# An operand sum of a Strassen-like product moved from VectorE to two DMA transfers

## The chip, the cores and the metric

The kernel runs on one core of one Trainium2 chip. The metric is the device time of one execution in microseconds. The engines are PE (matmul, with PEld for its weight loads), DVE (VectorE), ACT (ScalarE), POOL (GpSimd) and SP (SyncE, which here only issues transfers).

## The reference

An input `x` of 8 batches, 3008 rows and 256 columns goes through the real part of a two-dimensional Fourier transform and then through an MLP-Mixer layer. The last step, the channel mixing, is where the change lies.

```python
def _attn_ref(x):
    X = np.fft.fft(x, axis=1)
    X = np.fft.fft(X, axis=2)
    return X.real.astype(np.float32)

def _moe_ref(x, w_tok1, w_tok2, w_ch1, w_ch2):      # d_tok 256, d_ch 1536
    xt = x.transpose(0, 2, 1)
    h = np.maximum(xt @ w_tok1, 0.0) @ w_tok2
    u = x + h.transpose(0, 2, 1)
    h2 = np.maximum(u @ w_ch1, 0.0) @ w_ch2
    return (u + h2).astype(np.float32)
```

## The kernel before, in words

**Stages of a batch.** `fold` adds and subtracts mirrored rows and columns of `x` (tiles `xp` and `xm`) into `eo`. `front` turns `eo` into `ut`, the mixed tokens `u`, by small matmuls (`pz`, `pw`, `pt`, `py`, `pu`) with evictions on ACT and DVE. Then each batch has 6 chunks `c` of 512 tokens (448 in the last chunk of odd batches, 384 in that of even ones). For every chunk, `mm1` multiplies `ut` by w_ch1 in 12 steps `ct`, each of two 512-column matmuls into a PSUM tile `pc`, and ACT (in some chunks DVE too) evicts `pc` with a ReLU into `c1`. `pc` rotates through three banks.

**The second product.** `c1` times w_ch2 is done one chunk later. In most chunks (`seven(b, c)` true, 41 of 48) it is done by a scheme of seven block products in place of eight. `c1` is seen as four quarters (`quads`: a11, a12, a21, a22), split by channel half and by alternate blocks of 128 tokens. Four operand sums of 128x1536 elements, `s1` to `s4`, are formed on DVE by `sums`, and sums of the weight quarters (`b22`, `t1w` to `t4w`) were formed once on POOL by `weight_sums`. `mm2_seven` issues the products; each is 12 matmuls of 128 columns. Product 2 uses s2 and t2w, product 3 s1 and t1w, product 4 s3 and t3w, product 6 s4 and b22. DVE combines the results with `uT` (a DMA transpose of `ut`, three buffers) into `osb` (two buffers), and SP stores `osb`. The chunks for which `seven` is false are done by `mm2` with plain 256-column matmuls.

**Order of the work.** The schedule is written out by hand; nothing is reordered by a planner. The main loop runs over batches `b`, chunks `c` and steps `ct`; a slot is 12c + ct. In each slot it issues the `mm1` step of this chunk, and, by the tables below, the products and sums of the chunk before (`prev`):

```python
sum_at = {0: 1, 1: 2, 3: 4, 4: 3}
places = {0: 0, 1: -1, 2: 1, 5: 2, 6: 3, 8: 4, 10: 5, 11: 6}
```

Keys are `ct`. So the sum s3 is made at ct 4 and product 4 that uses it comes at ct 8. Between these, `take(nxt, 1)` spreads the 46 steps of the next batch's `front` over the batch. Each engine works through its own instructions in this order[...].

**POOL's fold.** From batch 2 on, `fold(b + 2)` runs on POOL in 26 pieces, 5 or 6 per chunk, all issued at ct 5. Ahead of them, a one-element copy into `hold` reads a sum, so that POOL begins when DVE has made it. When the last piece has been issued, `load_x` issues the loads of the batch after: two direct transfers into `xp` and two gathers into `xm`, all on POOL's queue. Batch 0 is set up differently: its fold and that of batch 1 are on DVE, and `weight_sums` is issued on POOL at slot 1, when w_ch2 (`wc2`) has been loaded.

Tiles of one `tag` with `bufs=1` share one place in SBUF; a new tile of the tag waits until the last reader of the old one is done. s1 to s4 have a tag each.

Of the kernel before, what the change touches and what calls it, by code (L numbers as in the profile page):

```python
# [36 lines left out]
def kernel(  # L37
# [51 lines left out]
    def tt(out_, a, b, op, eng=V):  # L89
        eng.tensor_tensor(out=out_, in0=a, in1=b, op=op)  # L90
# [4 lines left out]
    def act(out_, in_, scale=1.0, func=AFT.Copy, bias=None):  # L95
        kw = {} if bias is None else {"bias": bias}
        nc.scalar.activation(out=out_, in_=in_, func=func, scale=scale, **kw)  # L97
# [547 lines left out]
    def weight_sums():  # L645
        G.tensor_copy(out=wc2[:, :, D:D + 1], in_=wc2[:, :, P:P + 1])
        lo, hi = wc2[:, 0:NH], wc2[:, NH:NCT]
        b12 = lo[:, :, D:P:-1]
        G.tensor_copy(out=b22[:], in_=hi[:, :, D:P:-1])
        tt(t1w[:], b12, lo[:, :, 0:P], AT.subtract, G)  # L650
        tt(t2w[:], b22[:], t1w[:], AT.subtract, G)
        tt(t3w[:], b22[:], b12, AT.subtract, G)
        tt(t4w[:], hi[:, :, 0:P], t2w[:], AT.subtract, G)

    def mm1(b, c, c1, ct, on_v, cts=None):
        ut = state[b]["ut"]
        n = min(CW, S - CW * c)
        cts = cts or (ct,)
        pcs = [ps_out("pc", k % 5) if b + c == 0 and k % 5 < 2 else ps_mm("pc") for k in cts]
        for h in range(2):  # L660
            for pc, ct in zip(pcs, cts):
                nc.tensor.matmul(pc[:, 0:n], lhsT=wc1[:, h, ct * P:(ct + 1) * P],  # L662
                                 rhs=ut[:, c, h, 0:n], start=(h == 0), stop=(h == 1))
        for pc, ct in zip(pcs, cts):
            if ct not in on_v:
                act(c1[:, ct, 0:n], pc[:, 0:n], func=AFT.Relu)
            else:
                ts(c1[:, ct, 0:n], pc[:, 0:n], 0.0, AT.max)

    tail1 = const.tile([P, NCT, 64], FP16, tag="tail1")  # L670

# [21 lines left out]
    def quads(c1):  # L693
# [3 lines left out]
    def sums(c1, box, k):  # L697
        a11, a12, a21, a22 = quads(c1)
        box[k] = work.tile([P, NH, 2, P], FP16, tag=f"s{k}", name=f"s{k}", bufs=1)
        if k == 1:  # L700
            tt(box[1][:], a21, a22, AT.add)
        elif k == 2:
            tt(box[2][:], box[1][:], a11, AT.subtract)
        elif k == 3:
            tt(box[3][:], a11, a21, AT.subtract)
        else:
            tt(box[4][:], a12, box[2][:], AT.subtract)

    def product(dst, left, right, first):
        for a in range(2):  # L710
# [5 lines left out]
    def halves(ps):  # L716
        return ps[:, 0:2 * P].rearrange("p (a r q) -> p a r q", a=2, q=2)

    def mm2_seven(b, c, c1, uT, k, box):
        a11, a12, a21, a22 = quads(c1)  # L720
# [12 lines left out]
        def hi(i):  # L733
            return osb[:, i, :, P + 1:D + 1].rearrange("p a (r q) -> p a r q", q=2)[
                :, :, ::-1, ::-1]

        if k < 0:
            tt(q[:, 0], pa, u[:, 0], AT.add)
        elif k == 1:
            pb = ps_out("pb", 1)  # L740
            product(pb, a12, wc2[:, NH:NCT, 0:P], True)
            tt(lo(0), halves(pb), q[:, 0], AT.add)
        elif k == 2:
            product(box["a"], box[2], t2w, False)
            tt(q[:, 1], pa, u[:, 1], AT.add)
        elif k == 3:
            box["b"] = ps_out("pb", 1)
            product(box["b"], box[1], t1w, True)
        elif k == 4:
            product(box["a"], box[3], t3w, False)  # L750
            tt(q[:, 2], pa, u[:, 3], AT.add)
            tt(hi(1), halves(box["b"]), q[:, 2], AT.add)
        elif k == 5:
            product(box["a"], a22, t4w, False)
            tt(lo(1), pa, u[:, 2], AT.add)
# [49 lines left out]
    def take(g, n):  # L805
        for _ in range(n):
            next(g, None)
# [48 lines left out]
              36: 1, 39: 1}  # L856
    prev = uT = uT_next = None
    folding = left = 0
    for b in range(BB):
        nxt = front(b + 1) if b + 1 < BB else iter(())  # L860
        fold1 = fold(1, V) if b == 0 and BB > 1 else iter(())
        first, done = (24 if b == 0 else 5 + 12 * ((left + 5) // 6 - 1) if left else 0), 0
        for c in range(NCH):
            c1 = work.tile([P, NCT, CW], FP16, tag="c1", name="c1", bufs=2)
            if c == 5 and b % 2:
                G.tensor_copy(out=c1[:, :, 448:512], in_=tail1[:])
            box = {}
            joins = prev is not None and seven(*prev[0:2])
            on_v = ((1, 5, 8), ())[c] if b == 0 and c < 2 else () if joins else (0, 3, 6, 9)
            for ct in range(NCT):  # L870
                slot = NCT * c + ct
# [77 lines left out]
```

## Time and profile before

| | before |
|---|---|
| median of 3 runs | 601.85 us (601.52 to 602.42) |
| the profiled execution's own time | 601.77 us |
| its span | 599.8 us |
| PE, DVE, ACT, POOL busy | 582.5, 449.5, 390.2, 255.1 us |
| matmuls | 6273 |
| mean granted PE clock | 0.999 |
| moved by DMA | 55.69 MB |

A profile shows one execution. A row of it names the line, the engine, the operation and the tiles, with the time of each instruction, and in the columns after it the idle time of the engine just before and what ended it. Most VectorE and GpSimd additions carry the line of a helper (L90), and most ACT operations that of another (L97), so that tiles tell them apart.

### The profile page before, as it was taken

What the parts mean: (1) busy time and instruction counts of PE and PEld (TensorE: products, weight loads), DVE (VectorE), ACT (ScalarE), POOL (GpSimd) and SP (SyncE); (2) the same over time, 40 slices, a digit from 0 to 9 for tenths busy, and PEclk for the clock granted to TensorE, in tenths of its full rate; (3) what the DMA queues carried; (4) which work ended last, traced back from release to release, by engine and by line L of the source; (5) the groups of instructions that cost most, each with busy time, mean ns of one, the idle gap of its engine ahead of it and who ended that gap; (6) DMA issues with size and microseconds to landing.
All of it is one profiled execution on the core that took longest, in us unless ns stands there. A gap on an engine that the chain in (4) does not pass through costs nothing.

```text
span 599.8 us, 15331 instructions
## 1 busy us (share of the span) xinstructions
PE 582.5 (97%) x6273; PEld 417.8 (70%) x6273; DVE 449.5 (75%) x924; ACT 390.2 (65%) x753; POOL 255.1 (43%) x396
## 2 busy tenths in 40 slices
PE   3899999999999999999999999999999999999997
PEld 3756676677767776667767777677766777666776
DVE  8769879685898668766898668856688757966663
ACT  8764665478647865477656867568665786556662
POOL 8550545937555554626348444565555000000000
PEclk9999999999999999999999999999999999999999
DMA  8992822277138913394335753376133422323533
GB/s 158 207 192 61 170 50 53 61 149 119 37 71 121 149 37 68 78 181 54 68 84 91 135 89 55 67 147 113 37 60 80 93 55 55 77 61 77 93 72 88
DMA packets 83414, 55.69 MB, mean 93 GB/s; under 512 B 53778, under 2 KB 80082, under 8 KB 82578
## 3 DMA queue, kind: packets, MB, share of 16 engines
q1 hardware_dynamic: 76816, 36.82, 31.9%
q0 software_dynamic: 6208, 17.63, 16.2%
q8 instruction: 49, 0.80, 0.6%
q10 hardware_dynamic: 320, 0.26, 0.2%
q14 instruction: 21, 0.17, 0.1%
HBM read 35.26 MB, written 24.64 MB: 100 GB/s over the span
## 4 chain that ended last, share of the span: by engine, by line
PE 82%; DVE 1%; issue 0%; DVEq 0%
PE pc L662 36%; PE pa L712 17%; PE pb L712 13%; PE pu L566 6%; PE po L775 4%; PE pt L595 3%; PE pz L471 1%; PE py L538 1%; PE pw L512 1%; PE pw L508 1%; DVE s L90 1%; DVE osb L90 0%; DVE ut L90 0%; PE pz L496 0%; DVE q L90 0%
## 5 line engine op out<-in xcount | busy, mean ns | idle before, releaser
L97 ACT ACTIVATE c<-pc 128x512 f16<-128x512 f32 (+1 forms) x553 | 314.4, 591 | 156.2 <-PE pc L662 138.7
L662 PE MATMUL pc<-ut,wc 128*128 128x512 f16 (+1 forms) x1152 | 316.5, 374 | 1.2 <-DVE ut L90 1.2
L712 PEld LDWEIGHTS <-s 128*128 128x128 f16 x1968 | 123.5, 98 | 37.5 <-DVE s L90 0.6
L662 PEld LDWEIGHTS <-wc 128*128 128x128 f16 x1152 | 97.0, 98 | 50.7 <-issue 3.0
L712 PEld LDWEIGHTS <-c 128*128 128x128 f16 x1476 | 93.0, 97 | 27.8
L90 DVE TENSOR_TENSOR q<-pa,uT 128x256 f32<-128x256 f32 x123 | 52.5, 427 | 47.6 <-PE pa L712 47.5
L90 DVE TENSOR_TENSOR s<-c 128x1536 f16<-128x1536 f16 x82 | 80.7, 984 | 4.7 <-ACT c L97 4.7
L908 POOL COPY hold<-s 128x1 f16<-128x1 f16 x29 | 5.4, 187 | 173.5 <-DVE s L90 173.5
L90 DVE TENSOR_TENSOR osb<-pb,q 128x256 f32<-128x256 f32 x123 | 52.0, 422 | 23.8 <-PE pb L712 20.3
L90 DVE TENSOR_TENSOR ut<-pu,yt 128x512 f16<-128x512 f32 (+1 forms) x96 | 63.3, 672 | 0.8 <-PE pu L566 0.4
L90 POOL TENSOR_TENSOR eo<-sab 96x512 f16<-96x512 f16 x48 | 52.7, 1114 | 1.6
L566 PE MATMUL pu<-w2r,uu 128*128 128x512 f16 (+1 forms) x168 | 50.0, 379 | 0.3 <-DVE ut L90 0.3
L90 POOL TENSOR_TENSOR sab<-fa,fb 96x256 f16<-96x256 f16 (+1 forms) x72 | 46.7, 673 | 0.0
L90 DVE TENSOR_TENSOR s<-s,c 128x1536 f16<-128x1536 f16 x41 | 40.4, 986 | 0.0
L97 ACT ACTIVATE w<-pw 128x257 f16<-128x257 f32 x90 | 34.8, 387 | 8.4 <-PE pw L512 5.5
L90 DVE TENSOR_TENSOR s<-c,s 128x1536 f16<-128x1536 f16 x41 | 39.0, 952 | 0.0
L775 PE MATMUL po<-wc,c 128*128 128x256 f16 x288 | 35.4, 273 | 0.0
L712 PE MATMUL pb<-wc,c 128*128 128x128 f16 x492 | 34.4, 219 | 0.0
L712 PE MATMUL pa<-wc,c 128*128 128x128 f16 x492 | 34.4, 219 | 0.0
L712 PE MATMUL pa<-t2w,s 128*128 128x128 f16 x492 | 34.2, 219 | 0.1
L712 PE MATMUL pb<-t1w,s 128*128 128x128 f16 x492 | 34.2, 219 | 0.0
L712 PE MATMUL pa<-t4w,c 128*128 128x128 f16 x492 | 34.2, 219 | 0.0
(187 smaller groups left out, 728.0 us busy)
## 6 DMA issues: line engine op xcount, KB each, us to landing
out_dram<-osb SPq DMA_DIRECT2D x83, 256.0 KB
xp<-in_x_dram POOLq DMA_DIRECT2D x14, 408.0 KB, 6.4
out_dram<-osb SPq DMA_DIRECT2D x11, 192.0 KB
uT<-ut SPq DMA_TRANSPOSE x96
w2n<-in_moe_w_tok_dram POOLq DMA_DIRECT2D x2, 752.0 KB, 9.8
w1p<-in_moe_w_tok_dram POOLq DMA_DIRECT2D x2, 384.0 KB, 8.2
wc<-in_moe_w_ch_dram POOLq DMA_DIRECT2D x1, 768.0 KB, 15.3
xp<-in_x_dram POOLq DMA_DIRECT2D x2, 272.0 KB, 5.7
```

Of the source, the lines that this page charges most:

```text
L90: eng.tensor_tensor(out=out_, in0=a, in1=b, op=op)
L97: nc.scalar.activation(out=out_, in_=in_, func=func, scale=scale, **kw)
L471: nc.tensor.matmul(out_, lhsT=rows[:, half * P:half * P + P], rhs=tab, start=True, stop=True)
L508: nc.tensor.matmul(pw[:, 0:256].rearrange("p (h d) -> p h d", h=2)[:, :, 0:65], lhsT=zg[:, 0, g], rhs=td[:, 0:130].rearrange("p (h d) -> p ...
L512: nc.tensor.matmul(pw[:, 64:322].rearrange("p (h d) -> p h d", h=2)[:, :, 0:64], lhsT=zg[:, 1, g], rhs=td[:, 130:258].rearrange("p (h d) - ...
L538: nc.tensor.matmul(py[:, P * k:P * k + P], lhsT=w[:, 4 * c + k, o:o + P], rhs=tab[:, 4 * c + k, :], start=True, stop=True)
L566: nc.tensor.matmul(pu[:, 0:64 * nk], lhsT=uu[:, th, h, :], rhs=w2[:, th, :, 8 * c:8 * c + nk], start=(th == 0), stop=(th == 1))
L595: nc.tensor.matmul(pt[:, o:o + n], lhsT=hw[:, g, c], rhs=w[:, g, w0:w0 + n], start=(g == 0), stop=(g == NG - 1))
L662: nc.tensor.matmul(pc[:, 0:n], lhsT=wc1[:, h, ct * P:(ct + 1) * P], rhs=ut[:, c, h, 0:n], start=(h == 0), stop=(h == 1))
L712: nc.tensor.matmul(dst[:, P * a:P * a + P], lhsT=left[:, k, a, :], rhs=right[:, k, :], start=(first and k + a == 0), stop=(k == NH - 1), s ...
L775: nc.tensor.matmul(po[:, o:o + D], lhsT=c1[:, ct, ks * P:ks * P + P], rhs=wc2[:, ct, 0:D], start=(ct == 0), stop=(ct == NCT - 1))
L908: G.tensor_copy(out=hold[:], in_=pbox[3][:, 0, 0, 0:1])
```

## The change

It has five parts.

1. **The third sum by transfers.** For chunks with c below 5 in batches 1 to 7 (`by_dma`, 35 chunks), s3 is no longer made by DVE. `sum_start` issues on SP, at ct 7 of the chunk's own turn, a copy of a11 into s3; `sum_end` issues on POOL, at ct 9, a transfer that adds a21 into it. The sum is then used, as before, at ct 8 of the next chunk's turn. For the other six chunks of the scheme s3 stays on DVE.
2. **Signs.** [...]s2, s3 and s4 become sums where they were differences. The weight sums and the results change sign with them. `t2w` is now minus `t4w`'s first form: `weight_rest`, at slot 10 of batch 0, makes it by an ACT copy with scale -1, and then POOL subtracts a quarter of w_ch2 from `t4w`.
3. **Layout.** For chunks with c below 5 that use the scheme, `c1` is written so that each quarter is one contiguous run of 1536 elements in a partition (`blocked`). Evictions write, and products and sums read, through that view.
4. **Places.** s3 of the next chunk is now filled while s1 to s3 of the chunk before are in use. The three tags rotate (`homes`): the new s3 takes the place of the old s1, which product 3 reads last, at ct 6.
5. **POOL's order.** The fold's pieces of a chunk are halved: one half at ct 5, the other at ct 9, behind `sum_end`. `load_x` comes behind that second half. In the chunk after a load (`late_x`), from batch 2 on, 4 pieces are taken in place of 5; the last piece of the fold then falls in chunk 0 of the next batch. `hold` reads s4 in place of s3.

```diff
 def weight_sums():
-        tt(t1w[:], b12, lo[:, :, 0:P], AT.subtract, G)
-        tt(t2w[:], b22[:], t1w[:], AT.subtract, G)
+        tt(t1w[:], lo[:, :, 0:P], b12, AT.subtract, G)
         tt(t3w[:], b22[:], b12, AT.subtract, G)
-        tt(t4w[:], hi[:, :, 0:P], t2w[:], AT.subtract, G)
+        tt(t4w[:], lo[:, :, 0:P], t3w[:], AT.add, G)
+
+    def weight_rest():
+        act(t2w[:], t4w[:], scale=-1.0)
+        tt(t4w[:], t4w[:], wc2[:, NH:NCT, 0:P], AT.subtract, G)
...
+            if seven(b, c) and c < NCH - 1:
+                dst = blocked(c1)[:, :, ct].rearrange("p i a t -> p a i t")
+                src = pc[:].rearrange("p (a i t) -> p a i t", a=2, i=2)
...
+    homes = [1, 2, 3]
+
+    def new_sum(box, k):
+        t = homes[k - 1] if k < 4 else 4
+        box[k] = work.tile([P, NH, 2, P], FP16, tag=f"s{t}", name=f"s{k}", bufs=1)
...
         elif k == 3:
-            tt(box[3][:], a11, a21, AT.subtract)
+            tt(box[3][:], a11, a21, AT.add)
...
+    def sum_start(c, c1, box):
+        homes.append(homes.pop(0))
+        new_sum(box, 3)
+        nc.sync.dma_start(out=box[3][:], in_=quads(c, c1)[0])
+
+    def by_dma(b, c):
+        return c < NCH - 1 and b > 0
+
+    def sum_end(c, c1, box):
+        G.dma_start(out=box[3][:], in_=quads(c, c1)[2], accum_op=AT.add)
...
-                    if ct in sum_at:
-                        sums(prev[2], pbox, sum_at[ct])
+                    k = sum_at.get(ct, 3)
+                    if ct in sum_at and (k != 3 or not by_dma(*prev[0:2])):
+                        sums(*prev[1:3], pbox, k)
...
+                if by_dma(b, c):
+                    if ct == 7:
+                        sum_start(c, c1, box)
+                    if ct == 9:
+                        sum_end(c, c1, box)
                 if slot == 1 and b == 0:
                     weight_sums()
+                if slot == 10 and b == 0:
+                    weight_rest()
...
                         if joins:
-                            G.tensor_copy(out=hold[:], in_=pbox[3][:, 0, 0, 0:1])
-                        n = min(left, 6 if c == 5 or b < 2 else 5)
-                        take(fold2, n)
+                            G.tensor_copy(out=hold[:], in_=pbox[4][:, 0, 0, 0:1])
+                        n = min(left, 6 if c == 5 or b < 2 else 4 if late_x else 5)
+                        take(fold2, n - n // 2)
                         left -= n
-                        if left == 0 and folding + 1 < BB:
-                            load_x(folding + 1)
+                        late_x = False
+                if ct == 9 and n:
+                    take(fold2, n // 2)
+                    n = 0
+                    if left == 0 and folding + 1 < BB:
+                        load_x(folding + 1)
+                        late_x = True
```

More of the change, by code (lines that the diff above doesn't have):

```diff
@@ L664, in mm1 @@
         for pc, ct in zip(pcs, cts):
+            if seven(b, c) and c < NCH - 1:
+                dst = blocked(c1)[:, :, ct].rearrange("p i a t -> p a i t")
+                src = pc[:].rearrange("p (a i t) -> p a i t", a=2, i=2)
+            else:
+                dst, src = c1[:, ct, 0:n], pc[:, 0:n]
             if ct not in on_v:
-                act(c1[:, ct, 0:n], pc[:, 0:n], func=AFT.Relu)
+                act(dst, src, func=AFT.Relu)
             else:
-                ts(c1[:, ct, 0:n], pc[:, 0:n], 0.0, AT.max)
+                ts(dst, src, 0.0, AT.max)
     tail1 = const.tile([P, NCT, 64], FP16, tag="tail1")
@@ L691, in store, with blocked, quads, sums @@
                 in_=osb[64:128, 3, 0:D])
-    def quads(c1):
+    def blocked(c1):
+        return c1[:].rearrange("p c n -> p (c n)").rearrange(
+            "p (i c a t) -> p i c a t", i=2, c=NCT, a=2)
+    def quads(c, c1):
+        if c < NCH - 1:
+            v = blocked(c1)
+            return v[:, 0, 0:NH], v[:, 0, NH:NCT], v[:, 1, 0:NH], v[:, 1, NH:NCT]
         v = c1[:].rearrange("p c (a i t) -> p c a i t", a=2, i=2)
         return (v[:, 0:NH, :, 0], v[:, NH:NCT, :, 0], v[:, 0:NH, :, 1], v[:, NH:NCT, :, 1])
-    def sums(c1, box, k):
-        a11, a12, a21, a22 = quads(c1)
-        box[k] = work.tile([P, NH, 2, P], FP16, tag=f"s{k}", name=f"s{k}", bufs=1)
+    homes = [1, 2, 3]
+    def new_sum(box, k):
+        t = homes[k - 1] if k < 4 else 4
+        box[k] = work.tile([P, NH, 2, P], FP16, tag=f"s{t}", name=f"s{k}", bufs=1)
+    def sums(c, c1, box, k):
+        a11, a12, a21, a22 = quads(c, c1)
+        new_sum(box, k)
         if k == 1:
@@ L702, in sums @@
         elif k == 2:
-            tt(box[2][:], box[1][:], a11, AT.subtract)
+            tt(box[2][:], box[1][:], a11, AT.add)
         elif k == 3:
-            tt(box[3][:], a11, a21, AT.subtract)
+            tt(box[3][:], a11, a21, AT.add)
         else:
-            tt(box[4][:], a12, box[2][:], AT.subtract)
+            tt(box[4][:], a12, box[2][:], AT.add)
+    def sum_start(c, c1, box):
[6 more added lines that the diff above has]
+        G.dma_start(out=box[3][:], in_=quads(c, c1)[2], accum_op=AT.add)
     def product(dst, left, right, first):
@@ L719, in mm2_seven @@
     def mm2_seven(b, c, c1, uT, k, box):
-        a11, a12, a21, a22 = quads(c1)
+        a11, a12, a21, a22 = quads(c, c1)
         u = uT[:].rearrange("p (a i) h (q r) -> p (i h) a r q", a=2, q=2)
@@ L750, in mm2_seven @@
             product(box["a"], box[3], t3w, False)
-            tt(q[:, 2], pa, u[:, 3], AT.add)
-            tt(hi(1), halves(box["b"]), q[:, 2], AT.add)
+            tt(q[:, 2], u[:, 3], pa, AT.subtract)
+            tt(hi(1), q[:, 2], halves(box["b"]), AT.subtract)
         elif k == 5:
             product(box["a"], a22, t4w, False)
-            tt(lo(1), pa, u[:, 2], AT.add)
+            tt(lo(1), u[:, 2], pa, AT.subtract)
         elif k == 6:
@@ L858 @@
     folding = left = 0
+    n, late_x = 0, False
     for b in range(BB):
```

## The prediction

> **What bounds the kernel now.** I read the page's first part, then who waits for PE, then busy time in windows, and last the timelines of two places that the change touches.
>
> The page's busy times (share of the span, instructions) come first; under them, from the page's chain, the shares by engine:
>
> ```profile
> PE 582.5 (97%) x6273; PEld 417.8 (70%) x6273; DVE 449.5 (75%) x924; ACT 390.2 (65%) x753; POOL 255.1 (43%) x396
> ...
> PE 82%; DVE 1%; issue 0%; DVEq 0%
> ```
>
> The waits of PE alone (total us, times, longest):
>
> ```profile
> PE filler L399 <- DVE ident L84: 8.1, 1, 8.1
> PE pc L662 <- DVE ut L90: 1.2, 2, 0.9
> ```
>
> Two windows of 100 us (busy us of PE, PEld, DVE, ACT, POOL; clock; DMA share; GB/s):
>
> ```profile
> 0.00:100.00 100.00, 87.03 (x853) 60.67 (x854) 83.19 (x225) 66.12 (x131) 53.19 (x82) 1.00 0.71 131
> ...
> 200.00:300.00 100.00, 100.00 (x1122) 73.17 (x1120) 73.28 (x142) 67.87 (x134) 50.03 (x78) 1.00 0.49 84
> ```
>
> PE is the bound, and from 100 us on it is busy without a gap. A busy PE is not proof of pace, so I compared starts: back-to-back matmuls start 0.216 us apart for 512 columns and 0.056 us for 128. Beyond that pace PE loses some 3 us in all after 100 us. No edit removes a matmul, so 3 us is the most that any relief of another engine can give there. What can move the time much is a new wait of PE.
>
> **What the Trainium skill says.**
> - "DMA: Bandwidth & Descriptors", section "SWDGE vs HWDGE vs iDMA": accumulating is only possible on a transfer issued by GpSimd. That is why POOL must issue the second transfer, in order with its fold. No accumulating transfer is in this trace.
> - The same page, "Anatomy of one DMA — SWDGE (gpsimd) path": about 2.0 us plus bytes over 436 GB/s, 2.9 us for the 393 KB here (128 partitions of 3,072 bytes). The trace disagrees: 408 KB of xp take a median 6.4 us to land. The trace decides.
> - "Collectives: The Full Stack", "The bandwidth ceiling: the fold count and why AG ≠ RS ≠ AR": an add inside a transfer needs two source reads, so it moves at about half the rate of a copy. Not shown here; it sets my upper bound.
> - "SBUF — State Buffer", "Who interferes with whom": a VectorE instruction with two SBUF inputs and a GpSimd one that reads SBUF exclude each other. The trace agrees: an operand sum takes 0.95 us alone and up to 1.49 us beside GpSimd's `pad` operations.
>
> **Part 1: weights (once).** One of POOL's subtractions becomes an ACTIVATE of `t2w` from `t4w`, at slot 10 of batch 0. ACT is in order: the evictions of slots 11 and later stand behind it, and PE has three banks for `pc`. POOL's timeline of before, then ACT's:
>
> ```profile
> 36.83 0.23 POOL L646 COPY wc<-wc 128x12 f16<-128x12 f16 x1 [5.92 <-DMA wc<-in_moe_w_ch_dram]
> 37.13 0.82 POOL L649 COPY b<-wc 128x768 f16<-128x768 f16 x1
> 37.92 1.50 POOL L90 TENSOR_TENSOR t1w<-wc 128x768 f16<-128x768 f16 x1
> 39.50 1.64 POOL L90 TENSOR_TENSOR t2w<-b,t1w 128x768 f16<-128x768 f16 x1
> 41.10 1.51 POOL L90 TENSOR_TENSOR t3w<-b,wc 128x768 f16<-128x768 f16 x1
> ```
>
> ```profile
> 39.19 3.05 ACT L97 ACTIVATE c<-pc 128x512 f16<-128x512 f32 x6 [0.21 <-PE pc L662]
> ```
>
> POOL starts only when w_ch2 lands, at 36.83 us. Afterwards it runs b22, t1w, then t3w (39.50 to 41.0) and the first form of t4w (41.1 to 42.8, at the 1.72 us of today's t4w). ACT has evicted slot 10 at 40.3 and waits until 42.8. The copy itself takes 0.83 us (ACT's 768-element rows from SBUF are 832 and 934 ns): 43.7. Slot 11's eviction, begun at 40.16 today, ends at 44.3 (0.60 us each). PE's matmul for slot 14 needs that bank; it starts at 40.94 today, so PE is **3.4 us** late.
>
> Not all of it stays. DVE is behind PE here, because it folds batch 1 in the same stretch:
>
> ```profile
> 44.22 1.50 PE L775 MATMUL po<-wc,c 128*128 128x256 f16 x12
> ```
>
> ```profile
> 46.63 0.74 DVE L90 TENSOR_TENSOR osb<-po,uT 128x256 f32<-128x256 f32 x2
> ```
>
> The first DVE instruction that needs delayed PE work, `osb` at 46.63, has its input at 45.7. So 0.9 us is absorbed and DVE is 2.5 us late. From there DVE runs without a gap to the `ut` that PE waits for before chunk 2 (the 1.2 us above), with over 1 us of room at each later input. Everything behind follows: **+2.5 us**, bounds 0 (below nothing is excluded: nothing is removed from PE or ACT here) and 3.4. POOL's last subtraction, after the copy, hides behind some 16 us of free POOL time.
>
> **Part 2: the sum that DVE loses.** 35 chunks (c below 5, batches 1 to 7) lose one `s<-c` each: 35 x 0.95 = 33 us of DVE. It is off the path: PE waited for a sum 0.6 us in the whole run. Gain 0 to 1 us; I take 0. The blocked layout of c1, the swapped signs and the added access dimensions keep the element counts: evictions stay at 0.60 us, sums at 0.95. If they did slow, ACT at 65% and DVE at 75% cover them, so 0; a tenth more on each eviction would still leave ACT below PE's time.
>
> **Part 3: the transfers.** Each of those chunks issues, one chunk ahead, a copy on SP (slot 7) and an accumulating transfer on POOL (slot 9). The copy waits for ACT's first six evictions and for the t1w product that last reads the tile it reuses. Behind it on SP stand the uT transposes and the stores, which have most of a chunk to spare (uT is used a chunk and a half later, osb has two tiles). The accumulating transfer waits for the copy's landing; behind it on POOL stand the second half of the fold and the loads of x. The budget is tightest in batch 7, whose chunks are 9.9 us long:
>
> ```profile
> 556.51 0.83 PE L712 MATMUL pb<-t1w,s 128*128 128x128 f16 x12
> ...
> 567.93 0.83 PE L712 MATMUL pa<-t3w,s 128*128 128x128 f16 x12
> ```
>
> The copy can go at 557.3. SP's stores of 256 KB land a median 3.4 us after their issue by the completion records, so I put the copy's landing at 560.8. The t3w product needs the sum at 567.8: the accumulating transfer has **7.0 us**. By the same count the other chunks leave 8.1 us (c=1), 8.3 (c=0), 9.2 (c=3) and 10.7 or more (c=2, 4). Its time is unknown: from below 3.4 us, as a copy; from above 10 us, xp's 6.4 with a second read of some 2 us and a store in the way. I take 6, so nothing is late and the cost is 0.
>
> Moved with it: x is loaded behind the transfer (its 4 issues on POOL, two of 0.54 and two of 0.95 us). In batches 2 to 5 the load falls in c=0 near 10 us, the first gather lands some 8 us later, and the fold of c=1 waits for it; with two fold pieces (2.5 us) ahead, that chunk's accumulating transfer goes 0 to 3 us later than the copy allows. Against 8.1 us of room: 0 to 1 us, four times; I take 0.7 in all. Fold pieces that now run past the chunk's end can meet DVE's first sum (up to 0.5 us each, the 1.49 above); DVE gained 0.95 us per chunk and the t2w product leaves the sums 0.4 to 3 us, so 0.
>
> **Sum.** The profiled execution took 601.77 us (span 599.8, 2.0 around it), 0.08 below the median of the runs. 601.77 + 2.5 + 0 + 0.7 = **605.0 us**.
>
> **Rivals.**
> 1. The accumulating transfer is late in every short chunk. For it: two reads, and stores and transposes share its engines (DMA share 0.34 to 0.5). Against: xp lands in 6.4 us beside other loads. At 9 us batch 7 is short by 2 us per chunk (half of that on average, since a stall lengthens the next budget: 5 us), c=0 and c=1 by 0.8 (about 6 us): 615. At 10 us, 628.
> 2. Not slower: the t2w wait costs nothing. Place: slot 14 of batch 0. It decides once POOL's t4w is ready about 2.6 us sooner, so that PE's delay falls under the 0.9 us that DVE's lag takes up; an earlier landing of w_ch2 than 36.8 us would do that. Price 2.5 us back: 602.5 or, with the loads harmless, 601.8. Against: nothing ahead of that landing is changed.
> 3. DVE's relief shows: PE loses its small waits after 100 us, up to 3 us, and part 1 is absorbed too: about 600. Against: those waits are mostly not for DVE.
>
> **Numbers.** Forecast 0.64, rivals 0.23, 0.10 and 0.03. About 0.2% (1.2 us) is what a measurement of this kernel tells from no change. Slower by more: 0.64 + 0.23 = 0.87; within: 0.10; faster: 0.03. The range, 602.6 to 616, takes in part 1 from 0.9 us up and the accumulating transfer up to 9 us; it leaves out rival 3, most of rival 2 and the upper half of rival 1.
>
> **What would show it.** Right: ACT shows a wait of some 2.5 us for POOL's t4w ahead of `t2w`, PE a hole near 41 us, DVE about 33 us less busy with 35 fewer sums, and no wait of PE (or its weight load) for a DMA into `s`. Wrong: PE waits for `s<-c` transfers in batch 7 or in c=1 (rival 1), or no hole near 41 us (rival 2).

## The result and the profile after

The changed kernel takes **623.12 us** (median of 4 runs, 622.5 to 625.33) against 601.8 us: a ratio of **1.0353** with a 95% interval of 1.0324 to 1.0383. It is slower, as forecast, but by 21 us and not by 3, and the time lies above the range. The profiled execution is the longest of the four, 625.33 us.

The lines of the profile after that answer to those of before. First the page's busy times (share of the span, instructions), then PE's waits (total us, times, longest), then the two windows of 100 us in the same columns as before:

```profile
PE 589.7 (95%) x6273; PEld 419.8 (67%) x6273; DVE 433.4 (69%) x889; ACT 389.0 (62%) x754; POOL 305.0 (49%) x433
```

```profile
PE pa L747 <- DMA s<-c: 9.2, 4, 3.0
PE filler L399 <- DVE ident L84: 8.8, 1, 8.8
PE pa L747 <- DVE s L90: 6.1, 8, 3.0
```

```profile
0.00:100.00 100.00, 86.80 (x850) 60.06 (x851) 83.31 (x225) 66.46 (x131) 54.77 (x82) 1.00 0.69 129
200.00:300.00 100.00, 93.66 (x1005) 67.44 (x1003) 61.85 (x119) 60.91 (x122) 57.05 (x78) 0.97 0.69 145
```

The first 100 us are as before. Behind them PE, which had no gap, waits for the DMA-made sum four times and for DVE's sums eight times, and the clock falls below 1.00. The moved data rose from 55.69 to 83.23 MB. DVE has its 35 sums less and is not awaited less for it.

The length of each chunk, from its first `mm1` matmul to that of the next, says where the loss sits. Against `e17_pairs_late` below, which has the same code but no pair of transfers before batch 6 and makes `t2w` at slot 22, chunk c = 2 of batches 2 to 5 is longer by 4.8, 4.6, 2.2 and 6.3 us (17.8 us together), chunks c = 4 and 5 of these batches by 4.0, batch 1 by 1.1. Batches 6 and 7, whose pairs both kernels have, are not longer; against `e5_rest_later`, which has no pair at all, they are longer by 0.3 us together. Batch 0 isn't longer either, and is within 0.1 us of that of the kernel before.

One of the four chunks, instruction by instruction. POOL's timeline of batch 2 (start, duration, in brackets the idle time before and what ended it), then SP's, then PE's:

```profile
190.79 0.88 POOL L742 DMA_DIRECT2D s<-c  x1 [2.68 <-PE pc L665]
...
192.41 1.33 POOL L106 DMA_DIRECT2D xp<-in_x_dram  x2
194.04 0.97 POOL L109 DMA_INDIRECT xm<-in_x_dram,ix  x1 [0.30 <-issue]
195.32 1.19 POOL L109 DMA_INDIRECT xm<-in_x_dram,ix  x1 [0.30 <-issue]
...
203.39 1.14 POOL L90 TENSOR_TENSOR fa<-xp,xm 96x508 f16<-96x508 f16 x1 [5.59 <-DMA xm<-in_x_dram,ix]
204.50 1.92 POOL L90 TENSOR_TENSOR fb<-xm,xp 96x508 f16<-96x508 f16 x1
206.38 0.95 POOL L90 TENSOR_TENSOR sab<-xp,xm 96x8 f16<-96x8 f16 x1
208.05 0.99 POOL L742 DMA_DIRECT2D s<-c  x1 [0.72 <-PE pc L665]
```

```profile
193.11 1.31 SPq L692 DMA_DIRECT2D out_dram<-osb  x2
194.46 0.61 SPq L697 DMA_DIRECT2D out_dram<-osb  x1
198.80 0.52 SPq L736 DMA_DIRECT2D s<-c  x1
199.37 6.18 SPq L685 DMA_TRANSPOSE uT<-ut  x2
```

```profile
209.50 1.02 PE L665 MATMUL pc<-ut,wc 128*128 128x512 f16 x4
213.48 1.23 PE L747 MATMUL pa<-t3w,s 128*128 128x128 f16 x12 [2.96 <-DMA s<-c]
214.50 0.32 PE L508 MATMUL pw<-td,z 128*128 128x130 f16 x1
```

The completion records of the trace give the landings. Chunk c = 0's accumulating transfer is in place at 194.80. The two loads into `xp` and the two gathers into `xm` (1.6 MB) follow it and land from 198.59 to 205.49. The copy of c = 1 leaves at 198.80, in the midst of them, and lands at **207.46**, after 8.65 us. So the accumulating transfer leaves at 208.05 and lands at 213.43. PE stood before the product that needs the sum from 210.5 on. POOL itself was free at 207.3, so the fold is not what held it: the wait that the row puts down to `pc` ended with the landing of the copy, 0.6 us earlier.

Over all 35 pairs the copy takes a median of 2.83 us and the accumulating transfer 4.47 us; the copies of c = 1 in batches 2 to 5, beside a load, take 7.8 to 9.6 us. In batch 7, whose chunks are the shortest, every sum lands 2.2 to 3.8 us before its product.

The stall is only part of the price. Two windows (busy times as above, clock, DMA share, GB/s), one with the stall and one behind it (a share above 1 comes of counting a packet's whole time where it starts):

```profile
205.90:213.00 7.10, 4.62 (x49) 2.94 (x45) 2.89 (x4) 4.99 (x11) 6.38 (x10) 1.00 1.16 224
213.30:219.00 5.70, 5.52 (x49) 4.08 (x50) 1.38 (x4) 2.46 (x6) 5.32 (x8) 0.70 0.66 99
```

After the stall PE's clock is 0.70 in the mean: matmuls of 128 columns start 0.107 us apart for 3.4 us, in place of 0.056. The stalls of 3.0 to 3.1 us (three of them; counted between the starts of the matmuls on both sides, less their pace, which gives 0.1 to 0.2 us more than the waits in the rows) are each followed by such a stretch, which costs some 1.7 us more; those of 2.1 and 1.6 us are not. The Trainium skill's "TensorE: Matmul & The Clock Gate", section "Part 1: The HAM clock gate", says that the clock halves after an idle window of about 3.4 us; here less was enough. In every profile of this case the recorded clock changes only at points that lie whole multiples of 3.41 us apart, and what tells the cases apart is how much of one such stretch PE stands idle: over all kernels of this document, a stretch of which stalls (those above 0.5 us counted) took 0.64 or more was always followed by the half clock, and one with less than 0.60 never. So a stall of 2.13 us inside one stretch halved the clock (`e7_load_ahead`), and one of 3.08 us across two did not (`e1_five`). The 17.8 us are 13.0 us of waiting and, as the remainder, 4.8 us of slower clock.

### The profile page after: what moved, and what is told of

It is laid out like the page before. It is cut to its first block, busy times and chain, and to the rows that moved or that the text cites. A ratio compares the mean times of both kernels' runs of the same rounds, so it can differ in the third digit from the quotient of the medians.

```text
span 623.6 us, 15583 instructions
## 1 busy us (share of the span) xinstructions
PE 589.7 (95%) x6273; PEld 419.8 (67%) x6273; DVE 433.4 (69%) x889; ACT 389.0 (62%) x754; POOL 305.0 (49%) x433
## 2 busy tenths in 40 slices
DMA packets 93496, 83.23 MB, mean 133 GB/s; under 512 B 54898, under 2 KB 81202, under 8 KB 92658
## 5 line engine op out<-in xcount | busy, mean ns | idle before, releaser
L747 PEld LDWEIGHTS <-s 128*128 128x128 f16 x1968 | 124.3, 99 | 56.4 <-DMA s<-c 11.2
L742 POOL DMA_DIRECT2D s<-c x35 | 31.3, 895 | 134.4 <-ACT c L97 28.2
L90 DVE TENSOR_TENSOR q<-uT,pa 128x256 f32<-128x256 f16 x41 | 17.2, 419 | 59.0 <-PE pa L747 59.0
L90 DVE TENSOR_TENSOR osb<-pb,q 128x256 f32<-128x256 f32 x82 | 34.4, 420 | 28.5 <-PE pb L747 26.9
L90 DVE TENSOR_TENSOR s<-c 128x1536 f16<-128x1536 f16 x47 | 49.8, 1060 | 3.6 <-ACT c L97 3.6
L952 POOL COPY hold<-s 128x1 f16<-128x1 f16 x31 | 9.1, 293 | 86.7 <-DVE s L90 86.7
L90 POOL TENSOR_TENSOR sab<-fa,fb 96x256 f16<-96x256 f16 (+1 forms) x72 | 51.0, 774 | 0.0
L90 POOL TENSOR_TENSOR fa<-xp,xm 96x508 f16<-96x508 f16 x24 | 29.9, 1245 | 31.0 <-DMA xm<-in_x_dram,ix 31.0
L747 PE MATMUL pa<-t3w,s 128*128 128x128 f16 x492 | 35.2, 223 | 9.4 <-DMA s<-c 9.2
L90 DVE TENSOR_TENSOR q<-pa,uT 128x256 f32<-128x256 f32 x82 | 34.5, 421 | 13.7 <-PE pa L747 8.8
L90 DVE TENSOR_TENSOR yt<-py,sqy 128x512 f16<-128x512 f32 x48 | 30.7, 680 | 8.3 <-ACT sqy L97 8.2
```

Of the source, the lines that this page charges most:

```text
L742: G.dma_start(out=box[3][:], in_=quads(c, c1)[2], accum_op=AT.add)
L747: nc.tensor.matmul(dst[:, P * a:P * a + P], lhsT=left[:, k, a, :], rhs=right[:, k, :], start=(first and k + a == 0), stop=(k == NH - 1), s ...
L952: G.tensor_copy(out=hold[:], in_=pbox[4][:, 0, 0, 0:1])
```

## The experiments

Fourteen kernels were run, on five chips; the kernel before took 601.8 to 603.3 us on them, and each ratio is to its runs on the same chip. Two theories stood at the start. **Order**: the accumulating transfer is late because of what stands ahead of it on POOL's queue. **Shadow**: the copy is late because a load of x occupies the DMA engines. A third question was whether a pair costs something by itself, as in rival 1.

| run | time, us | ratio to before (95%) |
|---|---|---|
| after | 623.12 | 1.0353 (1.0324 to 1.0383) |
| e1_five | 638.89 | 1.0593 (1.0537 to 1.0649) |
| e2_behind | 628.3 | 1.0388 (1.0316 to 1.046) |
| e3_dve_sum | 603.72 | 1.0019 (1.0 to 1.0037) |
| e7_load_ahead | 653.19 | 1.0817 (1.0751 to 1.0884) |
| e8_not_in_load | 611.97 | 1.0154 (1.0129 to 1.0178) |
| e9_no_reload | 608.85 | 1.0121 (1.0103 to 1.0138) |
| e4_whole_fold | 642.29 | 1.0655 (1.0624 to 1.0685) |
| e5_rest_later | 603.25 | 1.002 (1.0013 to 1.0028) |
| e13_three_parts | 610.28 | 1.0116 (1.0086 to 1.0146) |
| e14_load_c5 | 609.99 | 1.0121 (1.0091 to 1.0151) |
| e16_late_pool | 607.49 | 1.0092 (1.0078 to 1.0105) |
| e15_all_undone | 609.79 | 1.013 (1.0113 to 1.0147) |
| e17_pairs_late | 603.13 | 1.0016 (1.0009 to 1.0022) |
| e18_split_early | 610.58 | 1.0134 (1.0112 to 1.0156) |

### Are the transfers the loss at all? e3_dve_sum

```
     def by_dma(b, c):
-        return c < NCH - 1 and b > 0
+        return False
```

> Edit: the third sum is on DVE in all chunks again; layout, signs, weights, the split of the fold, the 4 pieces and the places of the loads are those of the changed kernel. Both theories: no transfer stands behind the fold's wait and 27.5 MB are gone; POOL still waits for xm at c=1, which only delays the fold. 602 to 606 us. If it were above 610, the layout or the split fold would be the cause and both theories wrong.

603.72 us: the loss is gone to within 0.2%. Blocked layout, signs, weights, parted fold and late loads together cost about 1 us (0 to 2 by the interval).

### What stands ahead on the queue: e1_five, e2_behind, e7_load_ahead

`e1_five` takes five pieces of the fold after a load, so that the loads for batches 5 to 7 go out a chunk earlier, in c = 5.

```
-   n = min(left, 6 if c == 5 or b < 2 else 4 if late_x else 5)
+   n = min(left, 6 if c == 5 or b < 2 else 5)
```

> Edit: after a load of x the fold takes 5 pieces again, not 4, so that the fold of batches 2 to 4 ends in c=5 and the loads for batches 5 to 7 are issued there, a chunk and a half ahead of the fold that reads them; the load for batch 4 stays in c=0 of batch 2. Theory order (the fold of c=1 waits for x, and the accumulating transfer stands behind it on POOL): the stalls of PE in c=2 of batches 3, 4 and 5 go with their clock loss, that of batch 2 stays; 608 to 613 us, POOL's wait for xm from 31 us to about 6. Theory traffic (the added 27.5 MB slow all transfers, wherever they are issued): at least 618 us, with waits of PE for s in other chunks.

The order theory wanted 613 us at most; it took 638.89. PE waited 16.6 us for DMA-made sums, and the stalls moved with the load: from c = 2 to c = 1 in batches 3 to 5 (that is, to the pair issued in c = 0). Order has a small part in it: in batch 2 the copy lands at 207.50 and POOL, at work on the fold, issues the accumulating transfer at 209.52.

`e2_behind` puts all of the fold's pieces behind the accumulating transfer in the chunk after a load.

```
-   take(fold2, n - n // 2)
+   behind = n if late_x else n // 2
+   take(fold2, n - behind)
 ...
-   take(fold2, n // 2)
+   take(fold2, behind)
```

> Edit: in the chunk after a load all four fold pieces are taken behind the accumulating transfer; the loads stay where they are. Theory order: POOL still waits for xm, but the accumulating transfer of c=1 no longer stands behind that wait, and PE's waits at the t3w product go (9.2 us of waits for DMA s to under 2); the late uT of batch 5 stays; 609 to 614 us. Theory traffic: copy and accumulating transfer land late by themselves while x is loading (the copy of batch 2, c=1 landed 8.7 us after its issue), so at least half of the waits stay, 616 us or more.

628.3 us, and the stalls of c = 2 stay (11.2 us of waits). With POOL empty ahead of it, the transfer is still late, since its copy is. This speaks against order and for the shadow.

`e7_load_ahead` issues the loads at ct 5, ahead of the accumulating transfer of their chunk.

> Edit: the loads of x are issued at ct 5, ahead of the accumulating transfer of their chunk, in the same chunks as in the changed kernel. Theory order: the loads leave POOL 2 to 5 us earlier (they no longer wait for the copy to land), the fold of c=1 waits that much less, and PE's stalls in c=2 shrink by that much, from 3 us to 0 to 1: 606 to 613 us. Theory traffic: x now stands in front of the copy and the accumulating transfer of c=0 on the same engines, and PE waits for s in c=1 in place of c=2: 618 us or more.

653.19 us. In four of the five batches with a load, the accumulating transfer behind it on POOL's queue lands 11 to 18 us after its issue (6.2 us in batch 3, where the copy came late), and PE waits 33.0 us:

```profile
PE pa L747 <- DMA s<-c: 33.0, 6, 11.2
```

Loads behind the transfer, as in the change, do protect the chunk's own sum. They push the load onto the next one's.

### The shadow by itself: e8_not_in_load, e9_no_reload

```
     def by_dma(b, c):
-        return c < NCH - 1 and b > 0
+        return (c < NCH - 1 and b > 0 and
+                not (c == 1 and 2 <= b <= 5 or c == 2 and b == 1))
```

> The changed kernel, with the third sum left to VectorE in just five of its 35 chunks: c = 1 of batches 2 to 5 and c = 2 of batch 1, those whose copy leaves while x is loading (their stalls at the t3w product are 9.8 us of idle PE and some 4 us of slower clock after it; 1 more in batch 1). Theory (the loads of x are what delays the pair; outside them it costs nothing): PE's waits for the DMA-made sum fall from 9.2 us to under 1 us and the time to 606 to 611 us; what is left above 604 is the rows of uT late beside a load (3 us in batch 5) and the waits at the t2w product (4 us). Rival (every pair costs its share, by its traffic or by its place on the queues): 30 of 35 pairs are left, so 620 us.

611.97 us, 0.97 above the theory's figures and far from the 620 of the rival. Five of 35 pairs carried 11 us (12 by the ratios). PE's waits for a DMA-made sum are gone; left are those for DVE's sums:

```profile
PE pa L747 <- DVE s L90: 7.2, 7, 4.1
```

The 4.1 us are batch 5's. DVE's timeline there:

```profile
424.07 0.42 DVE L90 TENSOR_TENSOR q<-pa,uT 128x256 f32<-128x256 f32 x1 [5.13 <-DMA uT<-ut]
424.41 1.49 DVE L90 TENSOR_TENSOR s<-s,c 128x1536 f16<-128x1536 f16 x1
```

Sum 2 (`s<-s,c`) stands in order behind an addition that waits for `uT`. That transpose was issued at 407.38, beside the last load of x, and landed 16.60 us later. In `e5_rest_later`, where the load leaves POOL earlier in the chunk since it stands behind no transfer, the transposes beside it landed within 8.1 us.

In `e9_no_reload`, batches 3 and later reuse the tiles of batch 2:

```
     def load_x(b):
+        if b > 2:
+            x_tiles[b] = kept[0]
+            return
         new_x(b)
+        kept.append(x_tiles[b])
```

> The changed kernel with no transfer of x after the third batch's: batches 3 to 7 fold the tiles of batch 2 once more (so their part of the result is that of other data), all else as it is, all 35 pairs of copy and accumulating transfer too. Theory (the shadow of the loads): the copy takes under 3.2 us everywhere, PE has no wait for the DMA-made sum of chunk c = 1 in batches 3 to 5 (one may stay in batch 2, whose x is loaded), uT is never late, and the time is 605 to 610 us, with the waits at the t2w product of 0.6 us in chunks c = 4 and 5 unchanged. Rival (the pair is late by its own place and length, or by the fold's pieces ahead of it on POOL): 616 to 623 us.

608.85 us, and no wait for a DMA-made sum, with all 35 pairs in place. The copy's median is 2.80 us and its longest 4.86 (under 3.2 was expected); the transposes take 9.2 us at most. That is the shadow, shown from both sides. What makes the copy late inside it is not parted further: in the rows of batch 2, three stores stand ahead of the copy on SP's own queue, and they land from 204.25 to 206.40, 11 to 12 us after their issue. The load may slow the copy itself or the stores that it stands behind. What stays is a chain of waits for DVE:

```profile
PE pa L753 <- DVE s L90: 3.4, 8, 0.6
```

### The fold's second half: e4_whole_fold, e13_three_parts

```
-   take(fold2, n - n // 2)        # at ct 5
+   take(fold2, n)
 ...
-   take(fold2, n // 2)            # at ct 9
```

> The changed kernel, with a chunk's pieces of the fold all taken at ct 5, as before the change, and none left for ct 9; the load of x stays at ct 9 behind the accumulating transfer. Theory: the second half of the pieces is what runs beside VectorE's copy of one column of osb (1.97 us in place of 0.23) and makes sums 1 and 2 late: the waits at the t2w product in chunks c = 4 and 5 (six of 0.6 to 0.7 us) go, and the load leaves 1.5 to 3 us earlier against the copy of the next chunk, so its shadow costs a little less: 612 to 619 us. Rival (the pieces at ct 5 now hold the accumulating transfer back instead, as the change's order of issue supposes): PE's waits for the DMA-made sum grow beyond 9.2 us, 623 to 635 us.

The time went the rival's way, and past its 635: 642.29 us, with 24.1 us of waits for DMA-made sums. Ahead of the accumulating transfer stand four to six pieces, and in the chunk after a load the wait for x too. But my first point held: the waits at the t2w product in c = 4 and c = 5 are gone. DVE's copy of one column of `osb`, in the kernel before, in the changed kernel, in this one and in `e9_no_reload` (ns: shortest, median, longest):

```profile
L759 DVE COPY osb<-osb x41: 170/173/1202, 82.7 to 591.0; 128x4 f32<-128x4 f32 x41
```

```profile
L794 DVE COPY osb<-osb x41: 171/324/1967, 83.4 to 614.5; 128x4 f32<-128x4 f32 x41
```

```profile
L794 DVE COPY osb<-osb x41: 171/173/828, 82.8 to 635.3; 128x4 f32<-128x4 f32 x41
```

```profile
L800 DVE COPY osb<-osb x41: 171/552/1987, 83.0 to 597.2; 128x4 f32<-128x4 f32 x41
```

Four elements per partition take up to 1.97 us where POOL's pieces run beside them, and sums 1 and 2 stand behind. The Trainium skill's "SBUF — State Buffer", section "Who interferes with whom", has GpSimd and a VectorE instruction in its fast modes exclude each other for a whole instruction. The trace fits in part: 0.17 us alone and up to 1.97 us beside POOL, but the longest waits last over two or three POOL instructions, not one. In which mode the copy runs no run shows.

`e13_three_parts` is `e8_not_in_load` with the fold whole at ct 5 from batch 2 on.

> e8_not_in_load (612.0 us: third sum on VectorE in the five chunks beside a load of x) with, from batch 2 on, all of a chunk's fold pieces at ct 5, so that none is left to run beside the end of the chunk. Theory (the loss has three parts: the pair in the shadow of a load, the fold's second half beside VectorE's copy of a column of osb, and the rows of uT late in chunk c = 2 of batch 5): the second part goes too; the six waits at the t2w product of 0.5 to 0.76 us (3.9 us) fall under 1 us together, the copy of osb to under 0.3 us in the mean, 607.5 to 609 us; left over is batch 5, where PE still waits some 4.3 us for sum 2 and then runs 2.6 us longer at the lower clock. Rival 1 (traffic of the pairs makes sums 1 and 2 late, not the fold's place): 611 to 613 us. Rival 2 (the whole fold at ct 5 holds the accumulating transfer back): PE waits for the DMA-made sum again, 614 us or more.

610.28 us, against the 607.5 to 609 of the theory. Its profile is of an execution of 618.0 us, above the other five (607.1 to 613.3), and is read only for batch 0, below. The gain over `e8_not_in_load` (ratio 1.0116 against 1.0154, the intervals meet) is not settled by this.

### A part that the first profile hid: e5_rest_later, e16_late_pool

`e5_rest_later` is `e3_dve_sum` with `weight_rest` 12 slots later:

```
-   if slot == 10 and b == 0:
+   if slot == 22 and b == 0:
         weight_rest()
```

> Third sum on VectorE everywhere, as in e3_dve_sum (603.7 us), and weight_rest 12 slots later (slot 22 in place of 10), where POOL's t4w has long been written when ACT comes to it. Theory (part 1 is free because VectorE's lag takes up ACT's 1.18 us): same as e3_dve_sum, 603.7 us within 0.6. Rival (ACT's wait for t4w costs the 2.5 us of the prediction, hidden by a gain elsewhere): 601 to 602 us.

603.25 us, the same as `e3_dve_sum`: there part 1 cost no more than ACT's copy does at the later place. That place has a price too: in batch 0, c = 1 is 0.8 us shorter than in `e3_dve_sum` and c = 2 is 1.3 longer. That part 1 was nearly free is read from the kernel before: against it batch 0 is 0.1 us longer in the changed kernel and 0.3 in `e3_dve_sum`. But in `e14_load_c5` and `e13_three_parts` batch 0 was longer by 3 to 4 us, and ACT had waited 3.2 and 3.8 us for t4w, because w_ch2 had landed at 38.0 and 38.6 us there in place of 36.3 (both ran on one chip). So POOL's part was lengthened, on `e3_dve_sum`:

```
-   G.tensor_copy(out=b22[:], in_=hi[:, :, D:P:-1])
+   for _ in range(4):
+       G.tensor_copy(out=b22[:], in_=hi[:, :, D:P:-1])
```

> Third sum on VectorE everywhere, as in e3_dve_sum (603.7 us), with POOL's copy into b22 in weight_sums made four times in place of once: three more of 0.82 us each, so that everything of weight_sums behind it, the first t4w included, comes 2.46 us later. It stands for weights that land later: in the profiles of e13_three_parts and e14_load_c5 POOL began weight_sums at 38.60 and 38.05 us in place of 36.3 to 36.5, ACT waited 3.8 and 3.2 us for t4w in place of 1.2 to 1.4, and PE lost 2.7 and 2.1 us at slot 15 in place of 0 to 0.3. Theory (part 1 does cost what the prediction put there, once POOL is later than VectorE's lag can take up): ACT waits some 3.9 us, PE 2.5 to 3 us, and the time is 606 to 607.5 us. Rival (slot 15's loss comes of something else on that chip, and ACT's wait is taken up in any case): 603.3 to 604.5 us.

607.49 us: 3.8 us more than `e3_dve_sum` (4.4 by the ratios). ACT's row and PE's:

```profile
45.44 0.84 ACT L97 ACTIVATE t2w<-t4w 128x768 f16<-128x768 f16 x1 [4.54 <-POOL t4w L90]
```

```profile
PE po L811 <- ACT c L97: 3.4, 1, 3.4
```

Four points line up: with ACT waiting 1.18, 1.36, 3.24 and 4.54 us (the changed kernel, `e3_dve_sum`, `e14_load_c5`, this run), PE's matmuls around slot 15 start 0.6, 0.8, 2.7 and 4.0 us behind their pace. Past some 0.55 us of wait, each further microsecond of ACT's is one of PE's. In this run the clock halves behind the stall too, at 47.98 us.

### What stays: e14_load_c5, e15_all_undone, e17_pairs_late, e18_split_early

`e14_load_c5` brings the loads back to c = 5 (as in `e1_five`) on top of `e13_three_parts`, and moves the chunks left to DVE with them.

> e13_three_parts with five pieces after a load in place of four, so that the loads for batches 5 to 7 go back to c = 5 as before the change, and with the chunks left to VectorE moved with the loads (c = 0 of batches 3 to 5, c = 1 of batch 2, c = 2 of batch 1). Theory: the late rows of uT of chunk c = 2 in batch 5 come of the load for batch 7 in c = 0; with it in c = 5 the third part goes as well, 30 pairs stay, and the time is that of the same layout without pairs, 602.5 to 604.5 us. Rival (a pair costs something wherever it is, or the load makes another transfer late in its new place): 606 us or more.

609.99 us: a miss. Some 3 us of it are batch 0's, of the part just told. Without them:

> e14_load_c5 (610.0 us) with weight_rest at slot 22 in place of 10, 30 pairs left. Theory (the four parts of the loss are apart: pairs and other small transfers in the shadow of a load, the fold's second half, and ACT's wait for t4w where the weights land late): batch 0 then takes what it takes in e5_rest_later whatever the landing of the weights, and the 3 us that e14's profile lost in chunk c = 1 of batch 0 go: 604.5 to 607 us, what is left being the late rows of uT in batch 2 (2.3 us). Rival (the pairs cost 6 to 8 us by being there at all): 609 to 610.5 us.

Batch 1 began 2.3 us earlier than in `e14_load_c5`, as expected, but the time was the rival's, 609.79 us. Chunk c = 3 of batch 2 took 17.4 us in place of 13.5. POOL's timeline there and DVE's:

```profile
219.60 1.38 POOL L90 TENSOR_TENSOR sab<-fb,fa 96x252 f16<-96x252 f16 x1
220.93 0.99 POOL L742 DMA_DIRECT2D s<-c  x1
...
222.04 2.35 POOL L90 TENSOR_TENSOR eo<-sab 96x512 f16<-96x512 f16 x2
```

```profile
218.62 0.49 DVE L84 TENSOR_SCALAR uu<-uv 128x256 f16<-128x256 f32 x1
...
222.23 4.50 DVE L84 TENSOR_SCALAR uu<-uv 128x256 f16<-128x256 f32 x1
```

The copy had landed at 213.31; the accumulating transfer waited another 7.6 us for the fold's pieces ahead of it. And a TENSOR_SCALAR of this shape, which takes 0.29 us with no GpSimd instruction beside it, takes 4.50 us beside POOL's pieces. It is the second that PE waited for: the sum landed at 224.96, and the product stood until DVE was through. The half clock follows, at 227.36.

```profile
227.12 1.25 PE L747 MATMUL pa<-t3w,s 128*128 128x128 f16 x12 [2.08 <-DVE q L90]
```

To tell these from a price of every pair:

```
     def by_dma(b, c):
-        return c < NCH - 1 and b > 0
+        return c < NCH - 1 and b > 5        # weight_rest at slot 22
```

> The changed kernel with the pair of transfers only in batches 6 and 7 (10 of the 35 chunks), where no x is loaded and nothing is folded, the third sum on VectorE in the others; weight_rest at slot 22, so that the landing of the weights plays no part. Theory (a pair costs nothing where the DMA engines and POOL are free, however short the chunk): as e5_rest_later, 603.3 us within 0.8, and no wait of PE for a DMA-made sum in batches 6 and 7. Rival (each pair costs some 0.2 us of its own, 35 pairs then 7 us, which is what e15_all_undone keeps): 605 us or more.

603.13 us. Ten pairs in the shortest chunks, with no load and no fold beside them, cost nothing that shows: the ratio is 1.0016, and 1.002 without a pair (`e5_rest_later`).

`e18_split_early` is `e15_all_undone` with the fold parted again in c = 0 to 2.

> e15_all_undone (609.8 us) with the fold's pieces parted again between ct 5 and ct 9 in chunks c = 0 to 2 of batches 2 to 5, whole at ct 5 only from c = 3 on. Theory (what e15 kept is its own: with five pieces at ct 5 of c = 2 in batch 2, POOL issued that chunk's accumulating transfer at 220.9 us, 7.6 us after the copy had landed, and one TENSOR_SCALAR of VectorE took 4.5 us beside POOL's pieces; chunk c = 3 of batch 2 took 17.4 us in place of 13.5): chunk c = 3 of batch 2 is back near 13.5 us, 605 to 606.5 us. Rival (the 30 pairs cost this wherever the fold is): 609 us or more.

A miss in time, 610.58 us, and the figure is the rival's, but the rows are not. Chunk c = 3 of batch 2 is back at 14.3 us. In its place the pieces behind the transfer meet DVE in each of batches 2 to 5: four TENSOR_SCALARs of 2.7 to 2.8 us, and c = 3 in batches 3 to 5 is 1.5 us longer than in `e15_all_undone`. One of them, DVE's row and POOL's:

```profile
219.85 2.77 DVE L84 TENSOR_SCALAR uu<-uv 128x256 f16<-128x256 f32 x1
```

```profile
219.56 2.28 POOL L90 TENSOR_TENSOR sab<-fa,fb 96x256 f16<-96x256 f16 x3
221.46 1.00 POOL L90 TENSOR_TENSOR sab<-fb,fa 96x252 f16<-96x252 f16 x1
```

So the pieces either hold the accumulating transfer back (PE's waits for DMA-made sums rise from 9.2 to 24.1 us in `e4_whole_fold`, and are 0.8 in `e15_all_undone`) or run into DVE's next work. No placing tried here is free of both; before the change, `hold` set the whole fold into the stretch after DVE's last sum. Some 2 us more of this kernel's time are batch 1's, with no load beside them: the first accumulating transfer of all landed after 8.2 to 8.5 us in four of the kernels and after 4.9 to 5.9 in six others. The changed kernel and `e2_behind`, alike up to there, differ in this (5.70 and 8.33 us); what decides it is open. No version with more pairs came near `e17_pairs_late`, and none beat the kernel before.

## Why the prediction was wrong in size

**Why not faster: right. Slower: right by luck.** PE is the bound, and the 35 sums were off its path. But the 2.5 us that made the forecast "slower" came to 0.1, and what made the kernel slower is mostly the term that was put at 0.7. DVE was busy 16 us less, not 33: the remaining sums take 0.97 to 1.06 us in the mean in place of 0.95 to 0.99, and the copy of `osb` 22.9 us in place of 14.3.

**Part 1, +2.5 us: 0 in this run, though the mechanism is real.** ACT waited 1.18 us, not 2.5, PE lost 0.6 at slot 15, and DVE's lag took that up (PE's wait for `ut` at chunk 2 fell from 1.06 us to 0.21):

```profile
42.03 0.84 ACT L97 ACTIVATE t2w<-t4w 128x768 f16<-128x768 f16 x1 [1.18 <-POOL t4w L90]
```

Several terms were mis-sized. POOL began at 36.29 us, half a microsecond sooner than in the trace of before, and its t4w took 1.54 us, not 1.72, so that t4w was ready at 42.0 and not at 42.8. ACT was through with slot 10 at 40.85, not 40.3. And slot 14 does not need the bank of slot 11: in the first chunk `mm1` takes `pc` of ct 0, 1, 5, 6, 10 and 11 from the `ps_out` banks, so that PE had a bank more of room than I counted. Rival 2 named this place and an earlier landing of w_ch2, but asked for t4w about 2.6 us sooner; it came 0.8 us sooner, and the spare bank did the rest. `e16_late_pool` shows the forecast's side of that point.

**Part 3, the pair by itself: right, with room.** The accumulating transfer takes 4.47 us where I put 6, the copy 2.83 where I put 3.4. The accumulating transfer takes 1.6 times as long as the copy, fixed parts included; the page's fit in the prediction gave 2.9 us. The half rate behind my upper bound is what its page says of a collective between cores; no run here settles it for one transfer. Rival 1, late by itself in batch 7 and in every short chunk, is wrong though the time lies among its numbers: batches 6 and 7 lost nothing, in the changed kernel as in `e17_pairs_late`. Its sign of waits in c = 1 came true, but by the copies: the accumulating transfers of c = 1 took 4.95 to 5.44 us.

**"0 to 1 us, four times; I take 0.7 in all": this step failed.** It measured 17.8 us for the very loads that it named (4.8 of them in batch 5 by the late `uT`, the rest by the late sums), plus 1.1 in batch 1. I had asked what the two fold pieces ahead of the transfer cost, and let the copy land after 3.4 us in every chunk, the median of SP's stores. Beside a load that median doesn't hold: the copy took 8.65, 7.82, 8.10 and 9.58 us in batches 2 to 5. The trace of before had it: its three stores issued from 191.46 to 192.80 us, beside the load for batch 4, landed after 8.4 to 9.1 us by the completion records, and the transposes behind them after 7.8 and 8.7. Their rows:

```profile
191.46 1.30 SPq L684 DMA_DIRECT2D out_dram<-osb  x2
192.80 0.61 SPq L689 DMA_DIRECT2D out_dram<-osb  x1
193.46 4.73 SPq L677 DMA_TRANSPOSE uT<-ut  x2
```

They were harmless then, since nothing waited for them within a chunk. With 8.7 us for the copy and 4.5 for the accumulating transfer, the sum of my own working is 13.2 us from a copy that can go at the same place, against 11.5 us that c = 1 leaves (the 8.1 us of budget and the 3.4 of the copy). The forecast would have been a stall of at least 1.7 us, four times, and perhaps a slower clock behind it, for which the prediction had no term. In batch 2 it was 8.65 us for the copy, 0.6 to the next issue and 5.4 for the transfer: 14.6 us, 3.1 over the 11.5, which is the stall measured there.

The Trainium skill states what can do this in "DMA: Bandwidth & Descriptors", section "Queues, rings and completion order": an engine goes round the queues that have work for it, a packet at a time, so that a transfer on SP's queue shares the engines with what POOL's has in flight. The trace fits that: the DMA share is 0.96 from 190 to 206 us (0.86 before), and the copy takes three times as long. But the stores ahead of the copy on SP's own queue could do the same, and no run parts the two.

**"So 0" for fold pieces beside DVE's first sum: 4.0 us.** I priced the meeting of a piece and a sum (0.5 us each). What met the pieces was a copy of four elements, of 0.17 us, that stands ahead of the sum and was lengthened to 1.97; the trace of before shows it at up to 1.20. The reading behind the 0.5 us was off as well: the sums of 1.48 and 1.49 us stand beside GpSimd's `eo` additions, not its `pad`, and the longest sum took 3.08 us, beside GpSimd's copies into `w2r`.

**What stays open.** e14, e15 and e18 keep 8 us, of which the layout without pairs has 1.3. The chunk lengths put the rest into batches 1 to 5 (in e14 some 3 us into batch 0). The rows above name two ways for it, and batch 1's share comes in part of an accumulating transfer that was slow by itself; whether a placing of the 26 pieces exists that has neither is open. How often w_ch2 lands late enough for part 1 to cost is not known either: POOL began between 35.7 and 38.6 us over these kernels, the two latest on one chip.

## What to carry to other kernels

Price a new transfer not by the median of its kind but beside what else is in flight when it leaves: look in the trace for any transfer, however unimportant, that was issued at the same place, and take its landing. A transfer that something waits for within a few microseconds must not leave while a large load is in flight; moving the load behind it only hands the shadow to the next one. And when work on GpSimd is moved, look at which VectorE instructions it will stand beside: a very short one can pay the most.

## What the runs showed of the hardware

- In the changed kernel an accumulating SBUF-to-SBUF transfer of 128 x 3,072 bytes lands a median 4.47 us after issue (3.9 to 5.7; the first one took 8.2 to 8.5 us in four other kernels), a plain copy of the same size 2.83 us (2.6 at best); beside 1.6 MB of loads the copy takes 7.8 to 9.6 us. In `e7_load_ahead` an accumulating transfer queued behind such loads on the same queue takes 11 to 18 us in four of five batches.
- A VectorE copy of four elements went from 0.17 to 1.97 us, and a TENSOR_SCALAR of 256 elements from 0.29 to 4.50 us (`e15_all_undone`), beside back-to-back GpSimd instructions.
- PE's clock halved for 3.41 us wherever stalls took 0.64 or more of one of the 3.41 us stretches in which its record is cut, and never at less than 0.60. By length alone there is no line: 2.13 us halved it in `e7_load_ahead`, 3.08 us in `e1_five` did not.
